# Quartered activation loads, sums on VectorE, and an earlier operand for P6 in a retention + two-layer kernel

## The chip, the cores and the metric

The kernel runs on one core of a Trainium2 chip. The metric is device time in microseconds: before the change three runs took 1147.37, 1147.97 and 1148.45 us, median 1147.97.

## The reference, cut to what matters

Retention over 4 batches, 8 heads, 768 tokens of 64 features, followed by two feed-forward layers on the 3072 x 512 result (512 to 2048 to 512 each):

```python
for t in range(S):
    state = gamma * state + einsum('bhd,bhe->bhde', k[:, :, t], v[:, :, t])
    y[:, :, t] = scale * einsum('bhd,bhde->bhe', q[:, :, t], state)
x = y.transpose(0, 2, 1, 3).reshape(B * S, H * D)
h = x @ moe_w_in;  x = maximum(0.01 * h, h) @ moe_w_out
h = x @ moe2_w_in; out = (h - tanh(h)) @ moe2_w_out
```

Everything is float32. The kernel writes each operand of a feed-forward matmul as a high part (rounded to the matmul's input format) and a low part (the rest) and adds three products, high*high, high*low and low*high.

## The kernel before, in words

**Stages.** Attention comes first (to about 115 us), in 24 steps, s = 0 to 23, each one head pair p and one chunk c of 128 tokens. Then the first matmul of layer one, in 3 token blocks sb of two chunks and 8 groups g of two feature tiles, then its second matmul, then layer two.

**The seven products.** For each (sb, g) the first matmul is done as seven products P1, P2, P5, P6, P3, P7, P4 of 2 x 2 quarters in a Strassen-like scheme. The table PROD names for each the weight operand, the activation operand, the PSUM bank family and its due slot inside the group: P1 0, P2 1, P5 2, P6 4, P3 5, P7 10, P4 13; group g adds 7g, block sb adds 56 sb. One product is six matmuls of 128 x 128 by 512 columns (L638). The activation operands are B11, B21, T1, T2, B22, T3, T4; T1 to T4 are sums or differences of the raw quarters, made in place by `minus` (L319): T1 and T2 on VectorE, T3 (after B22) and T4 (after T3) on GpSimd. Each operand is split by `upper` (high part, ScalarE, L148) and `lower` (low part, VectorE, L154) into four buffers. `build_wg` makes the weight operands of a group the same way (A11/A12, S1/S2, S3/S4, N22), with nine buffers, of which seven stay.

**Results.** P1, P5 and P6 are copied out of PSUM by ScalarE (L645); P2, P3 and P7 are completed by a VectorE sum into a buffer "c" (L651), which ScalarE rectifies one product later (L627) and SP stores to DRAM as g1s (L628); P4 is rectified from PSUM. P1, P6, P7 and P4 of a group share one bank, P5 and P3 another.

**Conversion.** The weights come as 64-bit floats. A conversion unit loads 512 KB into a "raw" buffer (4 of them), takes the absolute value on ScalarE (L182) and does four VectorE steps (L186, L188, L191, L194). The 16 units of the first weights start at step 5 of attention; the others run later. A weight set g needs units 2g and 2g+1.

**Order of the work.** Everything is issued in program order per engine; an engine's queue is never reordered. The order comes from generators in queues: `loads` (raw activations of the next block), `conv` (conversion), `bg` (weight sets, and the operands of block 0), `bx` (operands of blocks 1 and 2). `run(queues, us)` (L123) takes work from the first queue that yields a cost until a budget is used up: 2.3 us per attention step, and per product 1.3 us less 0.7 for a sum. A generator that yields None is blocked; `settle` (L135) blocks until the tick counter has moved. In attention odd steps ask conv first, even steps bg. Ahead of a product whose weights or operand are not yet written out, a loop (L684) advances the tick and runs the queues until they are.

**Block 0 in attention.** `bg` holds operands B11, B21 and T1 of block 0, weight sets 0 and 1, then the other operands from T2 on. At the end of attention the T2 subtraction is issued, its splits are not.

**Loads.** `load_xq` waits until slot 38 of the block before (`now`) and until no conversion holds raw buffers (`raws`), issues the four quarter loads of 512 KB one behind the other on SP, and hands them over five ticks later. SP's queue also carries all g1s stores.

**Buffers.** Buffers of 128 x 512 float32 come from one first-in first-out list `free` (64 in attention, 95 afterwards). A buffer is given back when the last instruction that reads it is issued; the next owner's first write waits for that reader, a DMA store included. A weight set starts only with 10 free, an operand with 8.

Of the kernel before, what the change touches and what calls it, by code (L numbers as in the profile page):

```python
# [47 lines left out]
LEAD = 96  # L48
LAG = 2

W2_EARLY, SLOT_US, W2_US, G_AHEAD = 8, 1.3, 1.2, 5


# [11 lines left out]
NSB = NC // 2  # L65
# [4 lines left out]
def kernel(  # L70
# [12 lines left out]
    nc = tc.nc  # L83
# [17 lines left out]
    where, free, home = {}, deque((wp, f"z{i}") for i in range(N_ATT)), {}  # L101
    serial = [0]

    def alloc(nm, dt=F32, shape=(P, TB)):
        pool, tag = free.popleft()
        serial[0] += 1
        t = pool.tile(list(shape), dt, tag=tag, name=f"{nm}_{serial[0]}")
        home[id(t)] = (t, pool, tag)
        return t

    def give(*ts):
        for t in ts:
            _, pool, tag = home.pop(id(t))
            free.append((pool, tag))
# [3 lines left out]
    now, tick = [-1], [0]  # L118

    def run(queues, us):  # L120

        while us > 0:
            for queue in queues:  # L123
                cost = next(queue[0], "end") if queue else None
                if cost is not None:
                    break
            if cost is None:
                return 0.0
            if cost == "end":
                queue.popleft()  # L130
            else:
                us -= cost
        return us

    def settle():  # L135

        t = tick[0]
        while tick[0] == t:
            yield None
# [58 lines left out]
    def conversion(units, ready=None, ahead=RAW_BUFS - 1):  # L198

        while ready and not ready():  # L200
            yield None
        last = len(units)
        at = {}
        raws[0] += 1

        def load(n):
            if n < last:
                units[n].load()
                at[n] = tick[0] + LOAD_LEAD

        for n in range(ahead):
            load(n)
        for n in range(last + 2):
            if n >= 2:
                yield from units[n - 2].done(units[n - 2])
            if n < last:
                while tick[0] < at[n]:
                    yield None
                units[n].s1()
            if 1 <= n <= last:  # L220
                yield from units[n - 1].s2()
                load(n - 1 + ahead)
        raws[0] -= 1
# [35 lines left out]
    def build_wg(g):  # L259
        while g + NG not in UN or g not in UN or len(free) < 10:  # L260
            yield None
        a, b = UN.pop(g), UN.pop(g + NG)
        s12, s34 = alloc("s12"), alloc("s34")
        w = {}
        ts = [alloc("wg", F32R) for _ in range(7)]
        for i, (n1, n2) in enumerate((("A11", "A12"), ("S1", "S2"), ("S3", "S4"))):
            hi, lo = ts[2 * i], ts[2 * i + 1]
            w[n1], w[n2] = (hi[:, :H2], lo[:, :H2]), (hi[:, H2:], lo[:, H2:])
        w["N22"] = ts[6][:, :H2], ts[6][:, H2:]
        upper(ts[0], a)  # L270
        nc.vector.tensor_tensor(out=s12[:, :H2], in0=b[:, :H2], in1=b[:, H2:], op=ALU.add)
        yield 0.4
        nc.vector.tensor_tensor(out=s12[:, H2:], in0=s12[:, :H2], in1=a[:, :H2], op=ALU.subtract)
        yield 0.4
        yield from settle()
        upper(ts[2], s12)
        lower(ts[0], ts[1], a)
        yield 0.7
        nc.vector.tensor_tensor(out=s34[:, :H2], in0=a[:, :H2], in1=b[:, :H2], op=ALU.subtract)
        yield 0.4  # L280
        nc.vector.tensor_tensor(out=s34[:, H2:], in0=a[:, H2:], in1=s12[:, H2:], op=ALU.subtract)
        yield 0.4
        yield from settle()
        upper(ts[4], s34)
        lower(ts[2], ts[3], s12)
        yield 0.7
        upper(w["N22"][0], b[:, H2:], -1.0)
        lower(ts[4], ts[5], s34)
        yield 0.7
        lower(*w["N22"], b[:, H2:], -1.0)  # L290
        give(a, s12, b, s34)
        WG[g] = w, ts
        yield 0.4
# [4 lines left out]
    def load_xq(sb, at):  # L298
        while now[0] < at or raws[0]:
            yield None  # L300
        q = {}
        for nm, kh, th in (("B11", 0, 0), ("B21", 1, 0), ("B12", 0, 1), ("B22", 1, 1)):
            t = cm.tile([P, 2, TB], F32, tag="raw", name=f"xq_{sb}_{nm}", bufs=RAW_BUFS)
            nc.sync.dma_start(out=t, in_=x1s[2 * sb + th, 2 * kh:2 * kh + 2].rearrange("k p t -> p k t"))
            q[nm] = [t[:, 0], t[:, 1]]
        arrive = tick[0] + LOAD_LEAD
        yield 0.0
        while tick[0] < arrive:
            yield None
        XQ[sb] = q  # L310

    def build_xc(sb, part, done=None):
        while sb not in XQ:
            yield None
        q = XQ[sb]
        old = SPAN * sb - 7
        b11, b12, b21, b22 = q["B11"], q["B12"], q["B21"], q["B22"]

        def minus(eng, out, x, y):  # L319
            for kt in range(2):  # L320
                eng.tensor_tensor(out=out[kt], in0=x[kt], in1=y[kt], op=ALU.subtract)  # L321


        todo = (("B11", b11, "P1", None), ("B21", b21, "P2", (nc.vector, b11, b12, b11)), ("T1", b11, "P5", None),
                ("T2", b11, "P6", None), ("B22", b22, "P3", (nc.gpsimd, b12, b22, b12)), ("T3", b12, "P7", None),
                ("T4", b21, "P4", None))
        for nm, src, by, nxt in todo[:3] if part == 0 else todo[3:]:
            while sb and now[0] < old + PROD[by][3]:
                yield None
            if sb:  # L330
                for t2 in XC[sb - 1].pop(nm):
                    give(*t2)
            while len(free) < 8:
                yield None
            if nm == "T2":
                minus(nc.vector, b11, b22, b11)
                yield 1.3
            if not sb and nm in ("T1", "T2"):
                yield from settle()
            out = [(alloc("xch", F32R), alloc("xcl", F32R)) for _ in range(2)]  # L340
            for kt in range(2):
                upper(out[kt][0], src[kt])
            yield 0.0
            for kt in range(2):
                lower(*out[kt], src[kt])
                yield 0.7
            XC.setdefault(sb, {})[nm] = out
            if nxt:
                minus(*nxt)
                yield 1.3 if nxt[0] is nc.vector else 0.0  # L350
            if nm == "T3":
                minus(nc.gpsimd, b21, b11, b21)
        if done:
            done()

# [6 lines left out]
    with tc.tile_pool(name="at", bufs=2, reuse_waits="tile") as at, \  # L362
# [166 lines left out]
                del S[s - 1], S[s]  # L529

        conv = deque([conversion(conv_in)])
        bg = deque([build_xc(0, 0), build_wg(0), build_wg(1), build_xc(0, 1, free_x)])
        us = 0.0
        a_scale_q(0, nc.vector)
        a_scale_k(0, nc.vector)
# [10 lines left out]
        for s in range(len(steps)):  # L546
# [14 lines left out]
            if s >= CONV_FROM:  # L561
                us = run((conv, bg) if s % 2 else (bg, conv), min(us + ATT_US, ATT_US))
# [112 lines left out]
    conv.extend((conversion(conv2[:W2_EARLY], made(1)),  # L675
                 conversion(conv_out, made(2))))
    bg.extend(build_wg(g) for g in range(2, NG))
    bx = deque(build_xc(sb, part) for sb in range(1, NSB) for part in range(2))
    loads = deque(load_xq(sb, SPAN * (sb - 1) + 38) for sb in range(1, NSB))
    xleft = [(c, p) for c in range(2, NC) for p in range(NPAIR)]  # L680
    us = 0.0
    for i, (at_, sb, g, nm) in enumerate(stream):
        an, bn, bk, _ = PROD[nm]
        while g not in WG or bn not in XC.get(sb, {}):  # L684
            tick[0] += 1
            run((loads, bg, bx, conv), 0.01)
        product(sb, g, nm)
        now[0] = at_
        tick[0] += 1
        done, late[:] = late[:], []  # L690
        used = collect(sb, g, nm)
        for args in done:
            rectify(*args)
        if sb == NSB - 1 and nm == "P4":
            give(*WG[g][1])
        if xleft:
            c, p = xleft.pop(0)
            t = xw.pop((c, p))
            nc.sync.dma_start(out=x1s[c, p], in_=t)
            give(t)  # L700
        us = run((loads, bg, bx, conv) if sb or at_ % 2 else (loads, conv, bg, bx), min(us + SLOT_US - used, SLOT_US))
        if len(stream) - 8 <= i < len(stream) - 8 + G_AHEAD:
            load_g(i - len(stream) + 8)
        if len(stream) - 4 <= i < len(stream) - 2:
            split_g(i - len(stream) + 4, nc.vector)
        if i == len(stream) - 2:
            mm_out1(0)
# [101 lines left out]
    bg = deque([second_weights()])  # L809
    us = 0.0  # L810
    first_x = None
    for n in range(NT):
# [11 lines left out]
        if conv:  # L824
            us = run((conv,), min(us + (W2_US if n >= NM else 1.9), 1.9))
        else:
# [5 lines left out]
            if n >= max(first_x + 7, 3 * NM + 8):  # L832
                us = run((bg,), min(us + 1.3, 1.4))
# [83 lines left out]
```

## Time and profile before

| | |
|---|---|
| median of 3 runs | 1147.97 us |
| profiled execution | 1147.07 us, span 1145.3 us |
| TensorE | 1131.6 us busy (99%) |
| VectorE | 754.2 us (66%) |
| ScalarE | 592.6 us (52%) |
| GpSimd | 188.4 us (16%) |
| granted TensorE clock, mean | 0.997 |

The time of a run is about 1.8 us more than the span from the first to the last instruction. Busy time of TensorE is modelled and includes overlap of one matmul with the next, so 99% does not mean that nothing can be saved: the starts of products, their pitch and the named waits are read instead. "X <- ACT xch" means that a TensorE instruction writing bank X waited for ScalarE's instruction writing xch. A granted clock of 1.00 is 2.4 GHz, 0.5 is 1.2 GHz.

### The profile page before, as it was taken

What the parts mean: (1) busy time and instruction counts of PE and PEld (TensorE: products, weight loads), DVE (VectorE), ACT (ScalarE), POOL (GpSimd) and SP (SyncE); (2) the same over time, 40 slices, a digit from 0 to 9 for tenths busy, and PEclk for the clock granted to TensorE, in tenths of its full rate; (3) what the DMA queues carried; (4) which work ended last, traced back from release to release, by engine and by line L of the source; (5) the groups of instructions that cost most, each with busy time, mean ns of one, the idle gap of its engine ahead of it and who ended that gap; (6) DMA issues with size and microseconds to landing.
All of it is one profiled execution on the core that took longest, in us unless ns stands there. A gap on an engine that the chain in (4) does not pass through costs nothing.

```text
span 1145.3 us, 16466 instructions
## 1 busy us (share of the span) xinstructions
PE 1131.6 (99%) x6075; PEld 933.7 (82%) x6075; DVE 754.2 (66%) x1252; ACT 592.6 (52%) x1025; POOL 188.4 (16%) x168
## 2 busy tenths in 40 slices
PE   9999898999999999999999999999999999999998
PEld 6888687787888888888888888888888888888886
DVE  3578895665677574472564667677677677667765
ACT  5766565645665343252463455445445455455543
POOL 3232100102000000000000232232232232232221
PEclk9999899999999999999999999999999999999999
DMA  9996454674668694594672001100100100200100
GB/s 231 239 257 184 164 204 159 199 247 168 239 220 298 211 337 165 193 331 145 241 276 74 10 1 38 37 1 29 46 1 13 62 1 1 74 1 1 38 1 37
DMA packets 134448, 148.02 MB, mean 129 GB/s; under 512 B 57440, under 2 KB 86240, under 8 KB 134368
## 3 DMA queue, kind: packets, MB, share of 16 engines
q1 hardware_dynamic: 134080, 146.83, 38.7%
q8 instruction: 47, 0.77, 0.3%
q14 instruction: 33, 0.27, 0.1%
q10 hardware_dynamic: 288, 0.15, 0.0%
HBM read 96.61 MB, written 50.33 MB: 128 GB/s over the span
## 4 chain that ended last, share of the span: by engine, by line
PE 80%; DVE 2%; ACT 1%; issue 1%; DVEq 0%; ACTq 0%
PE acc L771 23%; PE h L757 23%; PE o L598 23%; PE X L638 7%; PE Y L638 3%; PE Z L638 2%; DVE xcl L154 1%; DVE c L651 0%; ACT c L627 0%; ACT xch L148 0%; DVE xq_B L321 0%; DVE gl L144 0%; DVE st L779 0%; ACT cv L182 0%; ACT gh L143 0%
## 5 line engine op out<-in xcount | busy, mean ns | idle before, releaser
L144 POOL TENSOR_TENSOR gl<-e,gh 128x512 fp32r<-128x512 f32 x95 | 122.9, 1295 | 698.0 <-ACT gh L143 646.5
L598 PE MATMUL o<-gh,wo 128*128 128x512 f32 x768 | 237.1, 389 | 0.0
L143 ACT ACTIVATE gh<-e 128x512 fp32r<-128x512 f32 x96 | 60.8, 633 | 219.9 <-DVE e L798 219.9
L598 PEld LDWEIGHTS o<-gh,wo 128*128 128x128 f32 x768 | 144.1, 188 | 30.1
L791 DVE SCALAR_TENSOR_TENSOR e<-e,h 128x512 f32<-128x512 f32 x96 | 66.0, 688 | 152.4 <-ACT e L789 152.4
L771 PE MATMUL acc<-w2h,gl 128*128 128x512 f32 x384 | 149.6, 390 | 0.0
L598 PE MATMUL o<-gl,wo 128*128 128x512 f32 x384 | 149.5, 389 | 0.1
L771 PE MATMUL acc<-w2l,gh 128*128 128x512 f32 x384 | 149.4, 389 | 0.0
L771 PE MATMUL acc<-w2h,gh 128*128 128x512 f32 x384 | 149.4, 389 | 0.0
L757 PE MATMUL h<-xkh,w2h 128*128 128x512 f32 x384 | 149.4, 389 | 0.0
L757 PE MATMUL h<-xkl,w2h 128*128 128x512 f32 x384 | 149.4, 389 | 0.0
L757 PE MATMUL h<-xkh,w2l 128*128 128x512 f32 x384 | 149.4, 389 | 0.0
L638 PE MATMUL X<-xch,wg 128*128 128x512 f32 x384 | 128.5, 395 | 7.6 <-ACT xch L148 4.0
L144 DVE TENSOR_TENSOR gl<-gr,gh 128x512 fp32r<-128x512 f32 x96 | 64.5, 686 | 98.6 <-ACT gh L143 97.1
L638 PEld LDWEIGHTS X<-xch,wg 128*128 128x128 f32 x384 | 72.7, 190 | 24.9 <-ACT xch L148 4.5
L771 PEld LDWEIGHTS acc<-w2h,gl 128*128 128x128 f32 x384 | 72.0, 188 | 15.6 <-DVE gl L144 0.4
L598 PEld LDWEIGHTS o<-gl,wo 128*128 128x128 f32 x384 | 72.1, 188 | 15.3 <-DVE gl L144 0.5
L757 PEld LDWEIGHTS h<-xkh,w2h 128*128 128x128 f32 x384 | 72.1, 188 | 15.1
L771 PEld LDWEIGHTS acc<-w2l,gh 128*128 128x128 f32 x384 | 72.1, 188 | 15.0
L757 PEld LDWEIGHTS h<-xkh,w2l 128*128 128x128 f32 x384 | 72.1, 188 | 15.0
L771 PEld LDWEIGHTS acc<-w2h,gh 128*128 128x128 f32 x384 | 72.0, 188 | 15.1 <-ACT gh L143 0.2
L757 PEld LDWEIGHTS h<-xkl,w2h 128*128 128x128 f32 x384 | 72.0, 188 | 14.9
(91 smaller groups left out, 1879.2 us busy)
## 6 DMA issues: line engine op xcount, KB each, us to landing
g1s<-c SPq DMA_DIRECT2D x96, 256.0 KB, 2.1
gr<-g1s SPq DMA_DIRECT2D x96, 256.0 KB, 4.8
raw<-in_moe_w_in_dram SPq DMA_DIRECT2D x32, 512.0 KB, 5.5
raw<-in_moe_w_out_dram SPq DMA_DIRECT2D x32, 512.0 KB, 4.3
w2s<-cv SPq DMA_DIRECT2D x32, 256.0 KB, 4.3
w2r<-w2s SPq DMA_DIRECT2D x16, 512.0 KB, 5.4
q<-in_q_dram SPq DMA_DIRECT2D x24, 256.0 KB, 4.0
k<-in_k_dram SPq DMA_DIRECT2D x48, 128.0 KB, 3.8
```

The lines of the kernel that those rows point to most:

```text
L143: nc.scalar.activation(out=hi, in_=src, func=AF.Copy)
L144: eng.tensor_tensor(out=lo, in0=src, in1=hi.bitcast(F32), op=ALU.subtract)
L154: nc.vector.tensor_tensor(out=lo, in0=src, in1=hi.bitcast(F32), op=ALU.subtract)
L598: nc.tensor.matmul(ACC[j], a, b, start=m == 0 and i == 0, stop=m == NM - 1 and i == 2)
L638: nc.tensor.matmul(ps, w[:, c], x, start=first and kt == 0 and i == 0, stop=kt == 1 and i == 2, skip_group_check=True)
L757: nc.tensor.matmul(h, a, b, start=kt == 0 and i == 0, stop=kt == NK - 1 and i == 2)
L771: nc.tensor.matmul(ACC[j], a, b, start=m == 0 and i == 0, stop=m == NM - 1 and i == 2)
L791: nc.vector.scalar_tensor_tensor(out=w, in0=u, scalar=C3, in1=h, op0=ALU.mult, op1=ALU.mult)
```

## The change

It has five edits. The raw activations of blocks 1 and 2 are loaded one quarter, two ticks, then the next. T3 and T4 are subtracted on VectorE, and each is charged 1.3 us in the planner. The operands of a block are built in three parts (B11, B21, T1; T2; B22, T3, T4), and for block 0 the T2 part stands ahead of weight set 1. A conversion unit starts only when three buffers are free. In block 0, conversion goes first in even slots only from slot 2 on.

```diff
+BG_FIRST = 2
+PARTS = ((0, 3), (3, 4), (4, 7))
...
             if n < last:
-                while tick[0] < at[n]:
+                while tick[0] < at[n] or len(free) < 3:
                     yield None
                 units[n].s1()
...
         for nm, kh, th in (("B11", 0, 0), ("B21", 1, 0), ("B12", 0, 1), ("B22", 1, 1)):
+            start = tick[0] + 2
+            while q and tick[0] < start:
+                yield None
             t = cm.tile([P, 2, TB], F32, tag="raw", name=f"xq_{sb}_{nm}", bufs=RAW_BUFS)
...
-                ("T2", b11, "P6", None), ("B22", b22, "P3", (nc.gpsimd, b12, b22, b12)), ("T3", b12, "P7", None),
+                ("T2", b11, "P6", None), ("B22", b22, "P3", (nc.vector, b12, b22, b12)), ("T3", b12, "P7", None),
                 ("T4", b21, "P4", None))
-        for nm, src, by, nxt in todo[:3] if part == 0 else todo[3:]:
+        for nm, src, by, nxt in todo[slice(*PARTS[part])]:
...
             if nm == "T3":
-                minus(nc.gpsimd, b21, b11, b21)
+                minus(nc.vector, b21, b11, b21)
+                yield 1.3
...
-        bg = deque([build_xc(0, 0), build_wg(0), build_wg(1), build_xc(0, 1, free_x)])
+        bg = deque([build_xc(0, 0), build_wg(0), build_xc(0, 1), build_wg(1), build_xc(0, 2, free_x)])
...
-    bx = deque(build_xc(sb, part) for sb in range(1, NSB) for part in range(2))
+    bx = deque(build_xc(sb, part) for sb in range(1, NSB) for part in range(3))
...
-        us = run((loads, bg, bx, conv) if sb or at_ % 2 else (loads, conv, bg, bx), min(us + SLOT_US - used, SLOT_US))
+        us = run((loads, conv, bg, bx) if not sb and at_ >= BG_FIRST and at_ % 2 == 0 else (loads, bg, bx, conv), min(us + SLOT_US - used, SLOT_US))
```

## Rows read from the trace of the kernel before

**Rows 1.** Stretches: length, busy time (instructions) per engine, granted clock, DMA share, GB/s

```profile
119.50:123.55 4.05, 0.01 (x1) 0.00 (x0) 3.36 (x7) 1.79 (x4) 0.14 (x1) 0.91 0.01 2
123.55:129.80 6.25, 6.25 (x14) 4.65 (x15) 3.60 (x6) 3.15 (x6) 0.00 (x0) 0.51 0.77 253
...
143.00:171.60 28.60, 28.60 (x128) 23.64 (x127) 25.90 (x53) 19.31 (x36) 0.00 (x0) 1.00 0.57 207
...
182.90:186.06 3.16, 0.17 (x2) 0.01 (x1) 1.95 (x5) 1.17 (x3) 0.00 (x0) 1.00 0.16 62
...
363.00:620.00 257.00, 257.00 (x1134) 212.81 (x1135) 140.63 (x244) 104.24 (x179) 0.00 (x0) 1.00 0.63 224
```

**Rows 2.** What TensorE waited for: total us, times, longest

```profile
PE X L638 <- ACT xch L148: 4.0, 1, 4.0
PE X L638 <- ACT P L645: 3.0, 1, 3.0
```

**Rows 3.** TensorE in order of time: start, length, instruction, at starts of products

```profile
115.12 0.50 PE L638 MATMUL X<-xch,wg 128*128 128x512 f32 x1
...
140.68 0.40 PE L638 MATMUL Z<-xch,wg 128*128 128x512 f32 x1
...
178.82 0.39 PE L638 MATMUL Z<-xch,wg 128*128 128x512 f32 x1
...
192.44 0.39 PE L638 MATMUL Z<-xch,wg 128*128 128x512 f32 x1
...
212.24 0.39 PE L638 MATMUL Z<-xch,wg 128*128 128x512 f32 x1
...
278.88 0.39 PE L638 MATMUL Z<-xch,wg 128*128 128x512 f32 x1
...
289.10 0.39 PE L638 MATMUL Z<-xch,wg 128*128 128x512 f32 x1
```

**Rows 4.** ScalarE in order of time, ahead of the first P6

```profile
122.35 0.63 ACT L627 ACTIVATE c<-c 128x512 f32<-128x512 f32 x1 [2.14 <-DVE c L651]
122.89 2.17 ACT L148 ACTIVATE xch<-x 128x512 fp32r<-128x512 f32 x4
```

**Rows 5.** VectorE in order of time, same stretch

```profile
115.50 1.29 DVE L321 TENSOR_TENSOR x<-x,x 128x512 f32<-128x512 f32 x2
116.71 1.79 DVE L191 SCALAR_TENSOR_TENSOR cv<-raw,cv 128x512 int32<-128x512 int32 x1
...
121.64 0.68 DVE L651 TENSOR_TENSOR c<-Z,P 128x512 f32<-128x512 f32 x1
```

**Rows 6.** SP's queue in order of time, at the raw loads of blocks 1 and 2

```profile
173.79 1.97 SPq L304 DMA_DIRECT2D xq_B<-x1s  x4
176.14 9.72 SPq L628 DMA_DIRECT2D g1s<-c  x3
...
254.82 0.36 SPq L250 DMA_DIRECT2D w2s<-cv  x1
255.22 2.23 SPq L304 DMA_DIRECT2D xq_B<-x1s  x4
```

**Rows 7.** The stores to g1s issued from 165 to 200 us: time to landing

```profile
DMA to landing us min/median/max: 2.0/2.0/7.9
```

**Rows 8.** VectorE in order of time, around the start of block 1

```profile
184.11 0.69 DVE L651 TENSOR_TENSOR c<-Y,P 128x512 f32<-128x512 f32 x1 [6.90 <-DMA g1s<-c]
...
203.65 3.86 DVE L154 TENSOR_TENSOR xcl<-xq_B,xch 128x512 fp32r<-128x512 f32 x3
```

**Rows 9.** GpSimd in order of time

```profile
116.33 3.31 POOL L321 TENSOR_TENSOR x<-x,x 128x512 f32<-128x512 f32 x2 [18.28 <-DVE x L321]
```

**Rows 10.** VectorE's groups, 114.5 to 360 us: count, busy, mean ns, idle before

```profile
L191 DVE SCALAR_TENSOR_TENSOR cv<-raw,cv 128x512 int32<-128x512 int32 x29 | 21.1, 728 | 0.7
...
L188 DVE TENSOR_SCALAR cv<-cv 128x512 int32<-128x512 int32 x29 | 12.4, 426 | 0.9
...
L154 DVE TENSOR_TENSOR wg<-s,wg 128x512 fp32r<-128x512 f32 x14 | 9.4, 688 | 2.3 <-ACT wg L148 2.3
```

## The prediction

> **What bounds the kernel now.** I read the page first: TensorE is busy 99% of the span, VectorE 66%, ScalarE 52%, GpSimd 16%. So only time in which TensorE stands, or runs at its lower clock, can be won. The stretches say where: from 363 to 620 us it issues 1134 matmuls of 512 columns in 257.0 us, 0.2266 us each, so a product of six takes 1.36 us [rows 1]. The list of what TensorE waited for has two entries of size: 4.0 us behind ScalarE's xch and 3.0 us behind ScalarE's copy P [rows 2].
>
> What a place costs I take from the starts of products in the first layer, since a lower clock counts there too [rows 3]. P1 of group 0 starts at 115.12, P2 of group 2, the 14th product, at 140.68: 25.56 us where 13 products need 17.68, so **7.9 us** lost. From there to 178.82 are 28 products in 38.14 us, 38.08 by the pitch: nothing lost. 178.82 to 192.44 are seven (9.52) in 13.62: **4.1** lost. 192.44 to 212.24 are 14 (19.04) in 19.80: **0.8**. 278.88 to 289.10 are seven in 10.22: **0.7**. Together 13.5 us; more than that this change cannot win.
>
> **First loss.** P6 of group 0 needs operand T2. The high half of T2 starts on ScalarE at 122.89, behind a rectify that began at 122.35 [rows 4]. That rectify waited for VectorE's P2 sum, which started only at 121.64, since VectorE had the two T2 subtractions from 115.50 and conversion steps ahead of it, the first of 1.79 us [rows 5]. TensorE stood 4 us and then ran 6.25 us at a granted clock of 0.51, the 1.2 GHz level, at 14 recorded matmuls [rows 1].
>
> **Second loss.** SP issues four loads of raw activations in 1.97 us from 173.79 and the next stores from 176.14 [rows 6]. The median store lands in 2.0 us, one needed 7.9 [rows 7]. VectorE's P3 sum, whose output buffer that store still reads, starts at 184.11 after 6.9 us of waiting [rows 8]; ScalarE and the next P6 stand behind it, 3 us for TensorE. The clock stays 1.00 there [rows 1].
>
> **Third.** GpSimd's subtractions slow VectorE beside them: the conversion step at 116.71 took 1.79 us [rows 5], the mean is 0.73 [rows 10]; three xcl take 3.86 us at 203.65 [rows 8], where this shape has a mean of 0.69. The GpSimd pair beside the first lasts 3.31 us [rows 9].
>
> **The change part by part.** I followed the planner's order by hand, with its own costs and ticks.
>
> *T2 ahead of the second weight set.* In attention the T2 subtraction moves to step 18 and its four splits to step 21, before the second set. They need 1.2 us on VectorE (two subtractions from 115.50, the next instruction at 116.71 [rows 5]) and about as much again for the low halves; they take slots that the second set and conversions had, and TensorE does not wait for them. P6 then follows P5 at once, and the 4 us and the low clock go. What is late next: the buffers. With T2's four in use, three are left after the second set takes nine, and attention copies leave one; the new test for three free buffers stops conversion at steps 22 and 23. So attention ends with the second set half made and conversion about one unit behind. This work moves into the first slots of layer one:
>
> - P1 ends near 116.8; ScalarE, at about 0.54 us per instruction [rows 4], copies it and makes the high part of S3/S4 until 118.0; VectorE its low part to 118.65, the P2 sum to 119.25, N22 to 119.6, the first low half of B22 to 120.2, four conversion steps (2.3 us from their means [rows 10]) to 122.5, and only then the second low half of B22, to 123.1. P3 starts at 115.12 + 4 x 1.36 + 0.2 = 120.7; its fifth matmul, due at 121.6, needs that half: **1.6 us wait**, restart included.
> - Then VectorE has the T3 and T4 subtractions (1.2 each), eight sums and low halves at 0.6, five conversion steps and two halves of S1/S2 ahead of the low half of group 2's A11, with 1.6 us idle for T4's high halves, which stand on ScalarE behind P5's copy and a rectify. I get 135.55 for its end. P1 of group 2 wants it at its third matmul, 133.6: **2.0 us wait**.
> - From 143 to 171.6 VectorE is busy 25.9 of 28.6 us [rows 1], so it has little to give to a TensorE that comes earlier. My hand order puts P1 of groups 3 and 5 0.4 and 0.8 us ahead of their weights; 0.33 us per set for ScalarE (2.3 us over 7 sets [rows 10]) makes this **2.0 us** over both.
>
> First loss after: 1.6 + 2.0 + 2.0 = 5.6 of 7.9, gain **2.3 us**. Bounds: all of it (+7.9) if VectorE keeps ahead by 2 us more than I reckon, and -7 if both new waits bring the low clock (a rival below).
>
> *The sums on VectorE.* T3 and T4 cost four subtractions per block, 0.6 apart as the two from 115.50 are [rows 5]: 2.4 us. They remove GpSimd's slowing: 1.06 us on one instruction of block 0 and 1.8 on three in block 1 are seen, at most the 3.31 us that the pair lasts. I take 2.2 and 0 net. The waiting sums queued behind them are P3 and P7; P4 needs P7's only three products later. The small losses of blocks 1 and 2, 0.8 and 0.7, stand at the slowed xcl; I let 0.5 go in each: **1.0 us**, bounds -0.5 (the new subtractions delay T3) and +1.5.
>
> The Trainium skill ("SBUF — State Buffer", "Who interferes with whom") calls the port pair of GpSimd and VectorE an exclusive lock whose loser blocks for the whole instruction. By that rule VectorE would get up to 3.3 us per pair back and the sum would be 1 us better per block; the 1.79 us instruction shows about 1.1 us lost to one of two GpSimd instructions, less than the rule's most.
>
> *One quarter at a time.* Four loads now start two ticks (2.7 us) apart. Conversion of the first weights ends in my order at slot 34, the loads start at slot 38 as before and the last is taken as there after 6 + 5 ticks, slot 49, which is when the first operand of block 1 may be overwritten. So nothing later waits. The P3 sum still reuses the buffer just stored, since the last weight set again leaves five buffers; a store behind at most one load of 512 KB lands in 2.0 to 4 us in place of 7.9, so VectorE waits some 2 us. Before, TensorE stood 3 us for a wait of 6.9, so about 4 are covered. Gain **3.9** of 4.1; bounds 0 and 4.1. In block 2 the loads come at 255.22, where the early conversion has just ended [rows 6]; one or two slots later plus six ticks puts the data at slot 107, where 105 was needed. B11 is due at 112, T2 at 116: 7.2 us of VectorE work and 2.4 of sums in 12.2 us, so two slots are spare, and each slot beyond costs 1.36 us.
>
> *Order of conversion and weights.* It differs only in the first slot; counted above. The later start of the second layer's conversion, 2 to 4 slots, lies in stretches where TensorE is the bound (257.0 busy of 257.0 [rows 1]): nothing.
>
> **Sum.** 2.3 + 3.9 + 1.0 = 7.2 us. The profiled execution took 1147.07 us with a span of 1145.3, so 1139.9. The median of the runs shown is 0.9 above it, which would give 1140.8. I say 1140.5.
>
> **Rivals.**
> - *The first loss goes whole.* For it: VectorE still idles 2.7 us from 143 to 171.6 [rows 1], and my steps miss their deadlines by 2 us or less. Against: it is 91% busy there, and one late step delays all behind it. Then 6 to 7.9 in place of 2.3: 1135 to 1137.
> - *VectorE becomes the bound.* Each weight set comes late until conversion is done, and the first stretch gives nothing: 3.9 + 1.0 less up to 2, 1143 to 1145.5. For it: the work carried over from attention. Against: in total VectorE has as much to do from 114 us on as before (11.1 us of differing work on both sides in my count).
> - *The loads still come together.* Ticks also run in the loop that waits for weights without real time passing; if TensorE's program waits there for group 6 or 7, several quarters are issued at once, the second loss stays, and with a first stretch that gives nothing the time is 1146 to 1148. My order has these sets ready three slots ahead.
> - *The clock falls at the new waits.* Slower: 3.0 us of standing left the clock at 1.00, 4.0 us did not [rows 1, 2]. If the waits at P3 and at P1 of group 2 reach 4 us, each costs 4 plus the 3.3 that the low clock cost before (7.9 less the standing and small gaps). Then 14.6 + 2.0 stand against 7.9, minus 8.7, with 4.9 won elsewhere: 1151. It decides from 2.4 us more backlog on VectorE at P3.
>
> **How the numbers follow.** My forecast (gain of 4.5 to 9.5) 0.56, first loss whole 0.18, VectorE the bound 0.14, loads together 0.06, clock falls 0.06. A measurement of this kernel cannot tell under 0.2%, 2.3 us, from no change. Faster 0.87, same 0.07, slower 0.06. The range 1134.5 to 1146 takes in the first three, with some of their tails left out.
>
> **What would show it.** P6 of group 0 starts within 0.3 us of P5's end; no 0.5 clock after 115 us. P3's wait names VectorE's xcl, 1 to 2 us; P1 of group 2 waits for wg, about 2. Four loads lie some 2.7 us apart, no store needs over 5 us there, and seven products from the P2 of group 6 take about 9.6 us. No subtraction on GpSimd, no xcl over 0.8 us beside one. It is wrong if a wait over 3 us stands in the first 20 products, or if the data of block 2 comes later than slot 109.

## The result and the profile after

The changed kernel took **1138.51 us** (median of four runs, 1138.35 to 1138.99) beside 1148.21 us for the kernel before on the same chip: ratio 0.9916, 95% interval 0.9904 to 0.9928. That is 9.7 us faster; the forecast was 1140.5 with a gain of 7.2.

In the profiled executions (1147.07 and 1138.51 us) the last matmul starts at 1141.18 before and at 1131.42 after, 9.76 us earlier. The span shrinks by only 8.6, since 5.3 us follow that matmul in place of 4.1; in the profiled executions of all the other kernels below they are 4.1. The other three runs of the kernel after have spans of 1136.6 to 1137.2 us for 1136.7, so they may share this longer end; why it is there stays open.

The first view is the stretches of the kernel after, with the columns of [rows 1]: length, busy time (instructions) of TensorE, of its weight loads, VectorE, ScalarE and GpSimd, granted clock, DMA share, GB/s.

```profile
119.50:123.55 4.05, 2.68 (x12) 1.93 (x11) 3.95 (x9) 2.14 (x4) 0.00 (x0) 1.00 0.54 209
123.55:129.80 6.25, 6.25 (x30) 5.14 (x29) 4.48 (x9) 4.21 (x8) 0.00 (x0) 1.00 0.42 159
143.00:171.60 28.60, 28.41 (x125) 23.17 (x124) 26.75 (x54) 19.69 (x38) 0.00 (x0) 1.00 0.51 180
```

The 4 us of standing and the clock of 0.51 are gone: 30 matmuls in the second stretch for 14. In the third VectorE is busy 26.75 of 28.6 us, 94%. All that TensorE still waits for between 114 and 360 us is VectorE, and the waits are small (total, times, longest):

```profile
PE Y L644 <- DVE xcl L156: 1.4, 1, 1.4
PE X L644 <- DVE wg L156: 1.3, 2, 1.1
```

TensorE of the kernel after in order of time (start, length), at the starts of products as in [rows 3]; the idle time before an instruction and who ended it stand in brackets:

```profile
115.02 0.50 PE L644 MATMUL X<-xch,wg 128*128 128x512 f32 x1
...
119.28 0.39 PE L644 MATMUL X<-xch,wg 128*128 128x512 f32 x1
...
123.08 0.50 PE L644 MATMUL Y<-xcl,wg 128*128 128x512 f32 x1 [1.37 <-DVE xcl L156]
...
134.95 0.73 PE L644 MATMUL X<-xch,wg 128*128 128x512 f32 x2 [1.12 <-DVE wg L156]
...
135.99 0.39 PE L644 MATMUL Z<-xch,wg 128*128 128x512 f32 x1
...
165.03 0.40 PE L644 MATMUL Z<-xch,wg 128*128 128x512 f32 x1
...
174.61 0.39 PE L644 MATMUL Z<-xch,wg 128*128 128x512 f32 x1
...
184.13 0.39 PE L644 MATMUL Z<-xch,wg 128*128 128x512 f32 x1
...
203.19 0.39 PE L644 MATMUL Z<-xch,wg 128*128 128x512 f32 x1
...
269.83 0.39 PE L644 MATMUL Z<-xch,wg 128*128 128x512 f32 x1
...
279.35 0.39 PE L644 MATMUL Z<-xch,wg 128*128 128x512 f32 x1
```

P6 of group 0 (119.28) follows P5 at once. Counted as the prediction counts, in products of 1.36 us:

| place | lost before | left, forecast | lost after |
|---|---|---|---|
| P1 of group 0 to P2 of group 2, 13 products | 7.9 | 3.6 | 135.99 - 115.02 - 17.68 = 3.3 |
| from there to P2 of group 5 (165.03), 21 | 0 | 2.0 | 29.04 - 28.56 = 0.5 |
| P2 of group 6 (174.61) to 184.13, 7 | 4.1 | 0.2 | 0 |
| 184.13 to 203.19, 14 (start of block 1) | 0.8 | 0.3 | 0 |
| 269.83 to 279.35, 7 (start of block 2) | 0.7 | 0.2 | 0 |
| sum | 13.5 | 6.3 | 3.8 |

13.5 - 3.8 = 9.7 us, and the first P1 comes 0.1 us earlier: the 9.76 of the last matmul.

VectorE of the kernel after in order of time, the instructions that answer to [rows 5] and [rows 8]:

```profile
118.55 0.68 DVE L657 TENSOR_TENSOR c<-Z,P 128x512 f32<-128x512 f32 x1
...
122.34 0.68 DVE L156 TENSOR_TENSOR xcl<-x,xch 128x512 fp32r<-128x512 f32 x1
...
134.21 0.68 DVE L156 TENSOR_TENSOR wg<-cv,wg 128x512 fp32r<-128x512 f32 x1
...
173.30 0.68 DVE L657 TENSOR_TENSOR c<-Y,P 128x512 f32<-128x512 f32 x1
...
174.23 0.42 DVE L273 TENSOR_TENSOR s<-cv 128x256 f32<-128x256 f32 x1
...
194.89 1.29 DVE L156 TENSOR_TENSOR xcl<-xq_B,xch 128x512 fp32r<-128x512 f32 x2
```

The P2 sum starts at 118.55 for 121.64; the P3 sum of group 5 at 173.30 has no wait in brackets, where the one of before had 6.90. **It stands ahead of the last weight set's first write, at 174.23.** Before, that write came at 176.80 and the P3 sum behind it, at 184.11. VectorE of the kernel before:

```profile
176.80 0.42 DVE L271 TENSOR_TENSOR s<-cv 128x256 f32<-128x256 f32 x1
```

A pair of xcl takes 1.29 us, 0.65 each; before, three took 3.86.

SP's queue of the kernel after, and the time to landing of the g1s stores issued from 165 to 200 us:

```profile
170.65 0.39 SPq L309 DMA_DIRECT2D xq_B<-x1s  x1
172.16 0.32 SPq L634 DMA_DIRECT2D g1s<-c  x1
172.57 0.39 SPq L309 DMA_DIRECT2D xq_B<-x1s  x1
...
179.14 0.39 SPq L309 DMA_DIRECT2D xq_B<-x1s  x1
```

```profile
DMA to landing us min/median/max: 2.0/2.1/4.7
```

The quarters come one at a time, with stores between them, and the slowest store needs 4.7 us where it needed 7.9 [rows 7]. The forecast's picture is all there. Whether it is also the cause had to be tried.

### The profile page after: what moved, and what is told of

The parts are those of the page before. It is cut to its first block, busy times and chain, and to the rows that moved or that the text cites. A ratio compares the mean times of both kernels' runs of the same rounds, so it can differ in the third digit from the quotient of the medians.

```text
span 1136.7 us, 16464 instructions
## 1 busy us (share of the span) xinstructions
PE 1126.8 (99%) x6075; PEld 932.5 (82%) x6075; DVE 753.2 (66%) x1264; ACT 594.1 (52%) x1025; POOL 169.5 (15%) x156
## 4 chain that ended last, share of the span: by engine, by line
PE 96%; DVE 2%; issue 1%; ACT 1%; DMA 0%; SPq 0%; DVEq 0%; ACTq 0%
PE acc L777 23%; PE h L763 23%; PE o L604 23%; PE X L644 11%; PE Y L644 5%; PE Z L644 3%; PE sc L489 2%; PE y L511 2%; PE y L507 2%; PE kTp L454 1%; PE qTp L468 1%; PE u L528 1%; DMA k<-in_k_dram 0%; ACT c L633 0%; DVE c L657 0%
```

## The experiments

The theory of the prediction: the early T2 brings 2.3 us at the start, the quartered loads 3.9 at the second loss, the VectorE sums 1.0 at blocks 1 and 2. The rival that grew out of the trace after: the early T2 shifts the order of the buffers, and the second loss goes by that. All times are medians, each with its ratio to the kernel before on the same chip.

**One part alone, on the kernel before.**

*Quartered loads only.*

```diff
+            start = tick[0] + 2
+            while q and tick[0] < start:
+                yield None
```

> The kernel before with the quartered loads alone. If the three losses are separate, as the prediction has it: the 4.1 us between the P2s of groups 6 and 7 go, the 7.9 us of the start and the 0.8 and 0.7 us of blocks 1 and 2 stay: 4 us faster. Rival, that the second loss is a late effect of the first (VectorE still behind from the start): it stays, and the time is that of before within 1 us.

Measured 1142.15 us, 0.9954 (0.9937 to 0.9971), 5.4 faster. The second loss is 0 for 4.1; the losses of blocks 1 and 2 stay (0.74, 0.72). The first loss is 6.7 us, 1.2 less than before, though the edit changes nothing there: TensorE stood 4.1 us in front of P6 and then had a granted clock of 0.73 from 123.55 to 129.80 us, where it had 0.51 before [rows 1]. So 1.2 of the 5.4 us are not the work of the quartering. The slowest store lands in 2.9 us and the P3 sum still waits for it, as the prediction had it. VectorE of this kernel:

```profile
177.96 0.69 DVE L654 TENSOR_TENSOR c<-Y,P 128x512 f32<-128x512 f32 x1 [1.91 <-DMA g1s<-c]
```

So in the old order quartering is worth the forecast's 4 us, by its mechanism.

*Sums on VectorE only.*

```diff
-  (nc.gpsimd, b12, b22, b12)
+  (nc.vector, b12, b22, b12)
-                minus(nc.gpsimd, b21, b11, b21)
+                minus(nc.vector, b21, b11, b21)
+                yield 1.3
```

> The kernel before with all sums on VectorE alone; T2 stays behind the second weight set. Theory 1, the order makes the first loss: T2's high half still stands behind the P2 sum and the conversion steps, P6 waits 2 to 3 us, about 1 to 2 us of the 7.9 come back, and with the 1.5 us of blocks 1 and 2 the gain is 2.5 to 3.5 us. Theory 2, GpSimd beside VectorE makes it: the two conversion steps take 0.7 us each, P6 waits 2 us or less and TensorE's clock does not fall, so 5 to 5.5 of the 7.9 us come back and the gain is about 7 us.

Measured 1148.77 us over ten runs, 1.0010 (1.0000 to 1.0019): no gain. Parts of it are large and cancel. P6 of group 0 waits 1.98 us in place of 4.0 [rows 2], at a granted clock of 1.00 from 119.5 to 129.8 us; blocks 1 and 2 lose nothing; but the start as a whole still loses 7.4 us for 7.9, as 4.5 of them now fall between groups 1 and 2; 1.0 comes at group 4, and the second loss grows to 6.1. VectorE and TensorE there, and the stretch behind the wait:

```profile
184.49 0.69 DVE L652 TENSOR_TENSOR c<-Y,P 128x512 f32<-128x512 f32 x1 [6.94 <-DMA g1s<-c]
```

```profile
186.43 0.79 PE L639 MATMUL X<-xch,wg 128*128 128x512 f32 x1 [3.03 <-ACT P L646]
```

```profile
185.50:192.30 6.80, 5.87 (x14) 4.61 (x15) 4.39 (x10) 4.45 (x9) 0.00 (x0) 0.50 0.30 117
```

VectorE's wait is that of [rows 8], and TensorE stands 3.0 us as before [rows 2], but this time the granted clock is 0.50 behind it, the 1.2 GHz level, where it stayed at 1.00 before. That makes the 2.0 us by which this loss is larger. **So the prediction's 3.0 us is no safe length to stand.**

*Early T2 only* (the three parts, the three free buffers, the order of conversion; loads together, T3 and T4 on GpSimd):

```diff
+BG_FIRST = 2
+PARTS = ((0, 3), (3, 4), (4, 7))
...
+                while tick[0] < at[n] or len(free) < 3:
...
+        bg = deque([build_xc(0, 0), build_wg(0), build_xc(0, 1), build_wg(1), build_xc(0, 2, free_x)])
```

> The kernel after with the four loads together again and T3 and T4 on GpSimd again: T2 ahead of the second weight set alone. Theory 1 (order): P6 does not wait, P3 waits about 1.4 us and P1 of group 2 about 1.1, the start gives some 4 us, the second loss (4.1) and the 0.8 and 0.7 us stay: 4 us faster. Theory 2 (GpSimd makes the first loss): GpSimd's pairs slow the VectorE work in front of P3, P7 and P1 of group 2, their waits reach 3 us and more, and the gain is under 2 us.

Measured 1139.21 us, 0.9926 (0.9911 to 0.9941): 8.3 us faster by itself, twice what was expected. The second loss is 0, **though the four loads go out together and a store behind them lands in 7.8 us**. SP and VectorE of this kernel:

```profile
170.58 1.97 SPq L306 DMA_DIRECT2D xq_B<-x1s  x4
```

```profile
101.24 1.46 DVE L188 TENSOR_SCALAR cv<-cv 128x512 f32<-128x512 f32 x1
...
173.54 0.68 DVE L653 TENSOR_TENSOR c<-Y,P 128x512 f32<-128x512 f32 x1
```

The P3 sum at 173.54 stands ahead of the last weight set here too, and waits for no store. Blocks 1 and 2 still lose 0.73 and 0.71. At the start the losses are 1.8 to group 2, then 0.7 and 1.3 at groups 3 and 4; T3 and T4 ran on GpSimd inside attention, from 95 to 102.4 us, beside which a conversion step took 1.46 us (101.24) where its like takes 0.42. GpSimd at that step, and ScalarE ahead of group 4:

```profile
99.58 2.84 POOL L323 TENSOR_TENSOR x<-x,x 128x512 f32<-128x512 f32 x2 [1.63 <-ACT x L511]
```

```profile
146.95 0.67 ACT L184 ACTIVATE cv<-raw 128x512 f32<-128x512 f32 x1 [2.03 <-DMA raw<-in_moe_w_in_dram]
```

There ScalarE waits 2.0 us for raw weights to convert, and VectorE then stands idle for 2.5 us, up to 148.17. So at group 4 it is not that VectorE had no time left.

**One part left out.** The kernel after with its four loads together again (the first diff taken back):

> The kernel after with the four loads of a block together again; T2 early and the sums on VectorE stay. Revised theory (T2's place moves the P3 sum ahead of the last weight set, so that no sum meets the buffer of the held-up store): a store still needs 7 to 8 us, no sum waits for it, and TensorE loses nothing between the P2s of groups 6 and 7: the time of after, about 1138.5. Theory of the prediction (the quartered loads take away the second loss): 3 to 4 us come back there, about 1142.

Measured 1137.66 us, 0.9911 (0.9896 to 0.9926), 0.85 below the kernel after (0.6 by the ratios). Its last matmul starts at 1131.56, as after (1131.42), and the losses are the same at each place; in the profiled executions the difference lies behind the last matmul (4.1 us for 5.3). SP's queue, the landing of the stores from 165 to 200 us, VectorE and ScalarE:

```profile
170.78 1.96 SPq L306 DMA_DIRECT2D xq_B<-x1s  x4
```

```profile
DMA to landing us min/median/max: 2.0/2.0/7.8
```

```profile
173.42 0.68 DVE L654 TENSOR_TENSOR c<-Y,P 128x512 f32<-128x512 f32 x1
```

```profile
180.69 0.42 ACT L152 ACTIVATE wg<-cv 128x256 fp32r<-128x256 f32 x1 [1.35 <-DMA g1s<-c]
```

A store is held up for 7.8 us and no sum meets its buffer. By the order in which this program takes buffers, that buffer (of the P7 sum of group 4) goes to the ninth and last buffer of the last weight set; the P3 sum takes that of P4 of group 3, stored long before. In the kernel before it is the P3 sum that takes the held-up buffer. The weight set writes its ninth buffer late, at 180.69: ScalarE waits 1.35 us for the store there, and TensorE loses nothing. **In the changed kernel quartering gives nothing.**

**The buffer mechanism by itself.** The kernel before with the loads of block 1 allowed from slot 35, still together:

```diff
-    loads = deque(load_xq(sb, SPAN * (sb - 1) + 38) for sb in range(1, NSB))
+    loads = deque(load_xq(sb, 35 if sb == 1 else SPAN + 38) for sb in range(1, NSB))
```

> The kernel before with the loads of block 1 allowed from slot 35 in place of 38, all four still together. Buffer theory: the wait needs both, a store behind 2 MB of loads and a buffer list just emptied by the last weight set; three slots earlier the stores that are delayed are those of buffers with a longer way back to reuse, VectorE waits under 3 us and TensorE not at all: the 4.1 us go. Rival, that 2 MB together always hold up a store for which TensorE ends up waiting: a wait of 2 to 3 us stays, at an earlier product.

Measured 1143.17 us, 0.9962 (0.9949 to 0.9975). The loads go out at 169.48, the second loss falls from 4.1 to 0.4, and the slowest store still takes 5.4 us. The order is that of before: the P3 sum stands behind the last weight set's first write (176.59) and takes the same buffer. VectorE:

```profile
180.24 0.69 DVE L651 TENSOR_TENSOR c<-Y,P 128x512 f32<-128x512 f32 x1 [3.23 <-PE Z L638]
```

The profile names TensorE's P2 product for this wait of 3.2 us, but the sum doesn't read it. The store that still reads the sum's buffer, issued at 175.93, needed 4.2 us and so landed at about 180.1: the sum waited for it. The expectation had under 3 us of waiting and no loss, so it is nearly met. The order alone does little harm; what counts is how long the store of the buffer that the sum takes is held up.

**Can the wait at P3 go too?** The kernel after with conversion first only from slot 6 on, and the same with the loads together:

```diff
-BG_FIRST = 2
+BG_FIRST = 6
```

> The kernel after with BG_FIRST 6 in place of 2: in slots 2 and 4 the operands go ahead of conversion. P3's second low half is then issued before the four conversion steps and P3 does not wait (1.6 us with restart). If single late steps set the waits: 1.5 us faster than after. If VectorE's work as a whole is the bound from 120 to 165 us: the wait comes back at P1 of groups 2 to 5 and the time is within 0.7 us of after.

> The kernel after with BG_FIRST 6 and the four loads together. With BG_FIRST 6 alone the start gained 1.7 us, and 3.7 us were lost at block 1, 2.4 at block 2, since the loads began 2.7 us later and were handed over six ticks after that. If the quartering's six ticks make those losses: they go, and the time is 1.5 us under that of the kernel after with the loads together, about 1136. If the later end of conversion makes them by itself: 2 us or more stay at block 1.

Quartered: 1142.18 us, 0.9950 (0.9934 to 0.9967), 3.7 slower than the kernel after. The wait at P3 is gone (1.7 us gained), but block 1 starts 3.8 us late and block 2 2.5: conversion ends later, the loads begin only at 173.33, and six ticks put the last quarter at 182.86. SP's queue:

```profile
173.33 0.41 SPq L309 DMA_DIRECT2D xq_B<-x1s  x1
...
182.86 0.41 SPq L309 DMA_DIRECT2D xq_B<-x1s  x1
```

Together: 1135.69 us, 0.9892 (0.9875 to 0.9908). The loads go out at 173.54, blocks 1 and 2 lose nothing, 1.3 is left at group 2 and 0.5 at group 5. The P2 sum of group 6 (175.67) now stands behind the last weight set's first write (175.33) and takes the buffer of the P3 sum of group 5, but the store of that buffer was issued at 173.13, ahead of the loads; it landed in 2.2 us, and the sum does not wait. Here the quartering of the change costs 6.5 us.

**Block 0's sums on GpSimd, the others on VectorE**, with slot 2 and with slot 6:

```diff
-  (nc.vector, b12, b22, b12)
+  (nc.vector if sb else nc.gpsimd, b12, b22, b12)
...
+                minus(nc.vector if sb else nc.gpsimd, b21, b11, b21)
+                yield 1.3 if sb else 0.0
```

> The kernel after with T3 and T4 of block 0 on GpSimd, of blocks 1 and 2 on VectorE. GpSimd takes the two pairs during attention, at about 95 and 100 us, since T2 is there early, and VectorE has 2.4 us less between 122 and 127 us. If single late steps set the waits: P1 of group 2 does not wait and the 0.5 at group 5 goes, 1.5 to 1.9 us faster than after. If VectorE's work as a whole is the bound: waits of about 2 us in sum at groups 3 and 4 as with T2 alone, the time of after within 0.7 us.

> Both of the two last edits on the kernel after. Single late steps: P3's and P1's waits both go, 3 to 3.5 us faster than after, about 1135. VectorE as a whole: it has 2.4 us less to do by group 5 than in the kernel after, so at most about that of the 3.7 us lost at the start comes back, 1136.5 to 1138.

With slot 2: 1138.52 us, 0.9917 (0.9902 to 0.9932), no different from after. (Its last matmul starts 0.76 us later than there, as its first P1 comes 0.8 us later, but 4.1 us follow it and not 5.3.) The wait at P1 of group 2 is gone, that at P3 stays, and 0.65 and 1.20 come at groups 3 and 4. The time is the one that the expectation gave for VectorE's work as a whole. The trace doesn't bear that reading out: as with the early T2 alone, ScalarE waits for raw weights ahead of group 4, 1.8 us up to 147.19, and VectorE then stands idle for 2.3 us. What makes the losses at groups 3 and 4 was not tried.

With slot 6: **1135.54 us**, 0.9891 (0.9877 to 0.9906), with the loads-together version above the best seen, 3.0 us under the kernel after. From the first P1 to the P2 of group 6 only 0.15 is lost; but that P1 comes at 116.12, 1.1 later. Then 1.0 is lost at the second place, up to the P2 of group 7. ScalarE waits for raw weights here too (1.7 us up to 146.93), at no loss. VectorE and SP at the second place:

```profile
177.11 0.69 DVE L657 TENSOR_TENSOR c<-Z,P 128x512 f32<-128x512 f32 x1 [2.70 <-DMA g1s<-c]
```

```profile
169.94 1.60 SPq L309 DMA_DIRECT2D xq_B<-x1s  x1
171.63 0.89 SPq L634 DMA_DIRECT2D g1s<-c  x2
172.62 1.26 SPq L309 DMA_DIRECT2D xq_B<-x1s  x2
```

A sum meets a stored buffer again (2.7 us; that store landed in 4.8), and two quarters go out together at 172.62.

**The same with the loads together:**

> The kernel after with BG_FIRST 6, T3 and T4 of block 0 on GpSimd, and the four loads together. In the same kernel with quarters a sum waited 2.7 us for a store of 4.8 and TensorE lost 1.0 there, so here the order puts a sum behind the held-up store. Buffer theory: a store of 7 to 8 us makes that wait 5 to 6 us and TensorE loses 2.5 to 4 us between the P2s of groups 5 and 6: 1137 to 1139. Theory that the second loss had nothing to do with loads: 1.0 us stays, 1135.5.

Measured 1143.88 us, 0.9965 (0.9952 to 0.9978), 8.3 slower than with quarters. In both the P2 sum stands behind the last weight set and takes the buffer of the P3 sum of group 5; here the store of that buffer goes out behind all four loads and is held up longer. What TensorE waited for, VectorE, the landing of the stores, and the stretch behind the wait:

```profile
PE X L641 <- DVE c L654: 5.0, 1, 5.0
```

```profile
181.93 0.69 DVE L654 TENSOR_TENSOR c<-Z,P 128x512 f32<-128x512 f32 x1 [6.97 <-DMA g1s<-c]
```

```profile
DMA to landing us min/median/max: 2.0/2.0/8.1
```

```profile
183.00:190.00 7.00, 5.45 (x13) 4.29 (x14) 3.72 (x8) 3.34 (x7) 0.00 (x0) 0.52 0.34 132
```

The expectation had too small a loss: TensorE stands 5.0 us, and the clock behind that, which it left out, is 0.52, the 1.2 GHz level. The place costs 7.7.

**Quarters by product slots** instead of ticks, so that none can go out together:

```diff
-            start = tick[0] + 2
-            while q and tick[0] < start:
+            start = now[0] + 2
+            while q and now[0] < start:
```

> The same kernel with quarters two product slots apart in place of two ticks. In the version with ticks two quarters were issued together at 172.6 us, since ticks also run in the loop that waits for weights. Spaced by slots no two quarters come together: stores land within 4 us, the 1.0 us at group 6 falls to 0.3 or less, and if block 1 gets its data in time this is 1134.5 to 1135, the fastest. If the last quarter is late instead, 1 to 3 us are lost at the first products of block 1.

Measured 1137.89 us, 0.9909 (0.9894 to 0.9924), 2.35 slower than by ticks (2.1 by the ratios, 0.7 by the last matmuls of the profiled executions). The second place loses 0.5 in place of 1.0, but a sum still waits 2.2 us for a store, the slowest store needs 5.0 us where 4 were expected, and the last quarter goes out at 180.17 and block 1 starts 1.7 us late.

## Why the prediction was right or wrong

**The start: right in its steps, one term too large.** P6 has no wait. The P2 sum starts at 118.55 (forecast 118.65), the last low half of B22 ends at 123.0 (123.1), and the wait at P3 is 1.37 us (1.6), behind the xcl that was named. P1 of group 2 waits 1.12 us for wg (2.0), whose low half starts at 134.21 and not at about 134.9. The mis-sized term is "2.0 us over both" for groups 3 and 5: 0.5 was lost, all at group 5. VectorE is nearly full there, as foreseen, but the hand order's misses of 0.4 and 0.8 us, with an allowance for ScalarE on top, were finer than a sum of some twenty steps can carry. The gain of the place is 4.1, not 2.3. The clock stayed at 1.00 in the stretches shown, with no new wait over 1.4 us. The rival on the clock took 3.0 us of standing as harmless, from one case [rows 1, 2]; with the sums alone on VectorE the same 3.0 us were followed by 0.50.

**The second loss: right in size by luck, wrong in cause.** "The P3 sum still reuses the buffer just stored, since the last weight set again leaves five buffers" is the step that failed. With T2 early, the P3 sum is issued ahead of the last weight set, and takes a buffer that nobody reads any more; the buffer just stored goes to the weight set, which writes it later. The early T2 alone ends the loss with a store at 7.8 us, and the whole change without quartering has the same losses as with it. So the 3.9 us that the prediction gave to the quartering came by another way, and quartering would have added nothing. The prediction costed the move only at the products beside it, not at the order of buffers 50 us later. That a held-up store together with an emptied list makes the loss is borne out: in the old order quartering removes it and loads at slot 35 leave 0.4 of it, with the sum still waiting 1.9 and 3.2 us. It comes back, larger, where a P2 sum behind the last weight set takes the buffer of a store issued behind four loads, and it stays away where that store goes out ahead of them. Which of the early T2's edits (the parts, the three free buffers, conversion first) moves the P3 sum ahead was not tried one by one.

**The sums on VectorE: near, by addition of opposites.** Alone they give no gain, in part because the clock fell at the second loss. In the changed kernel the loss of blocks 1 and 2 goes from 1.4 (early T2 only) to 0.0; the forecast let 0.5 stay. At the start they add VectorE work: with block 0's sums on GpSimd the 1.12 at group 2 is gone, though with slot 2 about as much is lost at groups 3 and 4. The prediction's reading of their cost in block 0 left one instruction out: beside the GpSimd pair of [rows 9] not one conversion step was slow but two, 1.79 us at 116.71 and 1.66 at 118.53, some 2 us in all, near the 2.2 that it took. "0 net" held for block 0 (the mixed kernel with slot 2 takes the same time); the 1.0 us for the others should have been 1.4. VectorE of the kernel before, the second of the two:

```profile
118.53 1.66 DVE L194 SCALAR_TENSOR_TENSOR cv<-raw,cv 128x512 int32<-128x512 int32 x1
```

The Trainium skill ("SBUF — State Buffer", "Who interferes with whom") has the loser of the port blocked for the whole of the other engine's instruction. The traces agree with that. In the kernel with the early T2 alone the step that began at 101.24 ended at 102.70, just behind the GpSimd pair (99.58 to 102.42); it lost 1.04 us, less than a whole GpSimd instruction, because the second of the pair was already running when it began. The 1.79 us step of the prediction began 0.4 us after its pair too [rows 5, 9], so its loss of 1.1 us says nothing against the rule.

**The loads: part right.** In block 2 "one or two slots later plus six ticks" cost nothing, as the spare slots said. That the quarters could bunch when ticks run in the wait loop was the rival at 0.06; in the kernel after they do not, in the mixed kernel with slot 6 two of them do. The price of six ticks where conversion ends later, 6.4 us over two blocks, was not foreseen.

**The total** was 2.0 us too high. At the last matmul the gain was 2.5 larger than the 7.2 (1.5 at groups 3 and 5, 0.3 before them, 0.5 at blocks 1 and 2, 0.2 at the second place); 1.2 of it was lost again behind that matmul, and 0.6 had been added for the median.

## What to carry to other kernels

A part of a change can look like the cause, with each row as forecast, and do nothing: leave each part out of the whole, not only put it into the old kernel. Where buffers go round in one list, moving one operand shifts which transfer each later writer waits for, so follow the list to its next low point. Spacing transfers out by a count of scheduling steps is paid for where the first of them starts late.

## What the runs showed of the hardware beyond that

- A store of 256 KB lands in 2.0 us in the median. With four loads of 512 KB issued together ahead on its queue the slowest took 5.4 to 8.1 us, with spaced ones 2.9 to 5.0. It costs time only where the buffer's next writer comes before the landing and TensorE soon needs that writer: 7.8 us of landing cost TensorE nothing where a late weight write had the buffer.
- How long TensorE stood did not settle what its clock did. After 3.0 us of standing the granted clock was 1.00 in the kernel before [rows 1, 2] and 0.50 with the sums alone on VectorE. After 4.0 us it was 0.51 in the kernel before and after 4.1 us 0.73, in the same stretch, with the quartered loads alone. After 5.0 us it was 0.52.
- A wait of VectorE for a held-up store, 6.9 to 7.0 us each time, cost 4.1 us with the clock at 1.00, and 6.1 and 7.7 us with the clock at its lower level.
